# The first transform of u with 64-row, 128-column stationaries, u stored by channels of 640, and one eviction for LN1's shift

## The chip, the cores and the metric

The kernel runs on one core of one Trainium2 chip. The metric is the device time of one execution in microseconds; lower is better. The core has five engines with instruction streams of their own: PE (TensorE, matmuls; its weight loads are listed as PEld), DVE (VectorE), ACT (ScalarE), POOL (GpSimd) and SP (SyncE, which here issues DMAs).

## The reference

u is one sequence of 2048 positions with 640 channels. Two blocks follow each other, each with an adaptive layer norm whose scale, shift and gate come from a condition vector c:

```python
mod = (_silu(c) @ w_mod).reshape(c.shape[0], 6, 1, -1)
sa, ca, ga, sb, cb, gb = (mod[:, i] for i in range(6))
h = _layernorm(x) * (1 + ca) + sa
x = x + ga * _A_ref(h, ...)      # S4: y = irfft(rfft(h) * rfft(K)) + h * Dskip
h = _layernorm(x) * (1 + cb) + sb
x = x + gb * _B_ref(h, w1, w3, w2)   # silu(h w1) * (h w3), times w2
```

K is the convolution kernel of the state space model, `real(sum_n C P dB)` with `P = exp(dt A l)`, for each channel over all 2048 positions. Everything is float32.

## The kernel before, in words

The long convolution is done as a product of transforms. The position is split as l = 64 a + b (a to 32, b to 64), and so is the transform: a first transform over a, for each b, into 32 frequencies f with a real and an imaginary part (64 outputs), then a second over b (`stage2`, line 571, from `uk`), then the product with K's transform, then the inverse. The host lays x out so that a tile of 128 rows holds four values of b, each with its 32 values of a; there are 16 tiles `xt[j]`, j being b // 4.

**The first transform of u** is `u_stage1(j)`, line 395. LN1 has been applied to the tile in place by `ln1_norm` (line 376: statistics on DVE, the root on POOL, one ACT activation for each tile at line 390). LN1's scale 1 + ca is folded into the gate on K's side, so the shift is added as r = sa / (1 + ca); a shift that is constant over a transforms into c1 times r, with c1 the column sums of the transform. Each of the tile's four b, rows 32q to 32q+31, is multiplied with `s1r`, 32 rows by 64 columns, in two halves of 320 channels, so a tile has eight matmuls (line 412), each on an eighth of the array: 32 rows by 64 columns, position (32q, 64 hh). Two PSUM tiles `pu` take the outputs: channel half hh on partitions 64 hh on, two b next to each other in each. `pu[0]` always has the tag Z, of which there is one buffer; `pu[1]` has A or B in turn. The shift is added in one of two ways:

- in `pu[0]` of even tiles, four more matmuls (line 404) of one row, `c1` by `rrow` (r as a row), start the accumulation, and ACT copies the result out (line 415, through `acopy`, line 138);
- in `pu[0]` of odd tiles and in `pu[1]` of all, DVE adds `shift`, c1 times r for all 128 partitions, while it moves the result out (lines 417, 418).

A DMA on SP's queue then stores `u` (two buffers) in `us` in DRAM (line 419), whose layout is [half, c, f, b, 320 channels]; c is the real or the imaginary part. `u_load` (line 550) reads it back into `uk` by blocks of 128 channels, in four parts for each block, with 64 partitions (b) for each c. The third block holds channels 256 to 383, which lie in both halves, so it needs two DMAs where the others need one. For the first block `u_load` is called at step 7 of the loop at line 777, for the others in `stage2`.

**The shift itself** is made in `mod_shift` (line 319), once the first five pieces of the modulation are there (`mod_early`, whose weights `w_mod` come by DMA). Five small DVE instructions give r as columns. Matmuls with the identity (line 330) bring r to 64 rows of `pr` (tag Z), and a DVE copy makes `rrow` (line 331). DVE multiplies c1 with r into columns (line 333), six matmuls turn them (line 339) and a DVE copy makes `shift` (line 341).

**What sets the order.** The program is traced in the order of the code; a planner then orders the instructions of PE and DVE before line 837 by their place and readiness. ACT is different: `act`, `acopy` and `act_set` (lines 133 to 141) keep each ACT instruction behind everything traced on ACT before it, so ACT runs strictly in program order. After `mod_shift` (line 751) come a table load, the exponentials of the first steps (`exps(0)`, `exps(2)`) with `ln1_norm(0)` and `ln1_norm(1)`, and the sines of step 0; tiles 0 to 3 of u come next, and the steps 0 to 5 of the loop at line 777 do two tiles each (line 808), followed by `ln1_norm` of later tiles. In one such step ACT also makes the sines and exponentials of K's tables, DVE multiplies the tables, PE forms K from them (`kgen`, line 522) and transforms it (`k_stage1`, line 540). From line 830 on the order of the convolution is written out by hand. The second block, matmuls listed under the helper line 102, fills the rest of the span.

At the very start SP issues `cT`, `prm` (the parameters), `misc` (small constants, in which also the selectors `selx` and `stepx` lie), `iota`, `ident` and the weights of the modulation, in this order (lines 229 to 236).

Of the kernel before, what the change touches and what calls it, by code (L numbers as in the profile page):

```python
# [17 lines left out]
P = 128  # L18
L = 2048
D = 640  # L20
F = 1728
NA, NB = 32, 64
DC = 128
# [6 lines left out]
KD = D // P  # L30
NFT = 14
WC = 384
# [5 lines left out]
def consts():  # L38

    a = np.arange(NA)[:, None]  # L40
    f1 = np.arange(NA)[None, :]
    ang = 2 * np.pi * a * (f1 + 0.25) / NA
    s1 = np.zeros((4, NA, 2, 4, NA))
    s1r = np.zeros((4, NA, 2, NA))
    for q in range(4):
        s1[q, :, 0, q, :] = np.cos(ang)
        s1[q, :, 1, q, :] = -np.sin(ang)
        s1r[q, :, 0] = np.cos(ang)
        s1r[q, :, 1] = -np.sin(ang)
# [23 lines left out]
    c1 = s1r.reshape(4, NA, 2 * NA).sum(axis=1, keepdims=True).repeat(NA, axis=1).reshape(P, 2 * NA)  # L73
# [5 lines left out]
    misc = np.concatenate([selx, stepx, s1r, c1, one4, toq, tog], axis=1)  # L79
    f = lambda v: np.ascontiguousarray(v, dtype=np.float32)  # L80
    return {"s1": f(s1), "s2": f(s2), "i1": f(i1), "i2": f(i2), "iota": iota, "misc": f(misc),
            "ident": np.eye(P, dtype=np.float32)}
# [25 lines left out]
def tile_kernel(ctx: ExitStack, tc: tile.TileContext, a):  # L108
    nc = tc.nc
    V, S, G, PE = nc.vector, nc.scalar, nc.gpsimd, nc.tensor  # L110

    dram = ctx.enter_context(tc.tile_pool(name="dram", bufs=1, space=DRAM))
    us = dram.tile([2, 2, NA, NB, D // 2], F32, name="us")
    zs = dram.tile([NDC, NB, 2, NA, DC], F32, name="zs")
    xs = dram.tile([NT, P, D], F32, name="xs")

# [1 line left out]
    ident = cp.tile([P, P], F32, name="ident")  # L118
    i2 = cp.tile([P, NA], F32, name="i2")
# [13 lines left out]
    def act(*args, **kw):  # L133

        return tc.keep_in_program_order(S.activation(*args, **kw))  # L135

    def acopy(out, in_):
        return tc.keep_in_program_order(S.copy(out, in_))  # L138
# [18 lines left out]
    s1 = kp.tile([P, 2, P], F32, name="s1")  # L157
    iota = kp.tile([P, NPH], I32, name="iota")
# [7 lines left out]
    uk = kp.tile([P, 3, NA, DC], F32, name="uk")  # L166
# [17 lines left out]
    rrow = pm_.tile([P, D], F32, name="rrow")  # L184
    shift = pm_.tile([P, D // 2], F32, name="shift")
    cols = pm_.tile([P, 7, KD], F32, name="cols")
    lt = pm_.tile([P, 2, D - DC], F32, name="lt")
    misc = pm_.tile([P, 9 * NA + 1 + P], F32, name="misc")
    selx, stepx = misc[:, :NA], misc[:, NA:4 * NA]
    s1r, c1, one4 = misc[:, 4 * NA:6 * NA], misc[:, 6 * NA:8 * NA], misc[:, 8 * NA:8 * NA + 1]  # L190
    toq, tog = misc[:, 8 * NA + 1:8 * NA + 1 + P], misc[:, 8 * NA + 1 + P:]
    tiny = pm_.tile([P, 1], F32, name="tiny")
    V.memset(tiny, -1e-35)

# [31 lines left out]
    d0 = slice(0, DC)  # L226
    d1 = slice(DC, D)
    prma = a["prm"].rearrange("i n d -> n i d")
    nc.sync.dma_start(cT, a["c"])
    S.dma_start(ldt, a["log_dt"].broadcast_to([P, D]))  # L230
    nc.sync.dma_start(prm[:, :, d0], prma[:, :, d0])
# [87 lines left out]
    def mod_shift():  # L319

        sa, ca, ga, zero, inv, r, gs = (cols[:, i] for i in range(7))
        V.tensor_scalar(ca, ca, 1.0, None, op0=OP.add)
        V.tensor_scalar(zero, ca, 0.0, 1e-18, op0=OP.is_equal, op1=OP.mult)
        V.tensor_tensor(ca, ca, zero, op=OP.add)
        V.reciprocal(inv, ca)
        V.tensor_tensor(r, inv, sa, op=OP.mult)

        pr = psS.tile([P, 2, 512], F32, name="pr", tag="Z", bufs=1).rearrange("p a b -> p (a b)")
        for k in range(KD):
            PE.matmul(pr[:64, k * P:(k + 1) * P], r[:, k:k + 1].broadcast_to([P, 64]), ident, start=True, stop=True)  # L330
        V.tensor_copy(rrow[:64], pr[:64, :D])
        rc = pm_.tile([P, WC], F32, name="part", bufs=2)[:, :KD * 2 * NA].rearrange("p (k c) -> p k c", k=KD)
        V.tensor_tensor(rc, bc(c1, 1, KD), bc(r, 2, 2 * NA), op=OP.mult)
        ps = psS.tile([P, 512], F32, name="ps", tag="pk", bufs=1)
        for k in range(KD):
            for hh in range(2):
                lo, hi = max(k * P, hh * 320), min(k * P + P, hh * 320 + 320)
                if lo < hi:
                    PE.matmul(ps[hh * 64:hh * 64 + 64, lo - hh * 320:hi - hh * 320], rc[:, k],
                              ident[:, lo - k * P:hi - k * P], start=True, stop=True, tile_position=(0, hh * 64))  # L340
        V.tensor_copy(shift, ps[:, :320])

    def mod_gate():

# [44 lines left out]
            x = xt[2 * p + i]  # L389
            act(x, x, AF.Identity, scale=rs[:, 1, i:i + 1], bias=rs[:, 2, i:i + 1])  # L390

    usw = us.rearrange("h c f b d -> (h c f) b d")
    usr = us.rearrange("h c f b d -> h c b f d")

    def u_stage1(j):


        x = xt[j]
        u = hpz.tile([P, 4, D // 2], F32, name="u", bufs=2)
        pu = [psS.tile([P, 2, 512], F32, name="pu", tag=t, bufs=1) for t in ("Z", "AB"[j % 2])]  # L400
        one = j % 2 == 0
        for q in range(2 if one else 0):
            for hh in range(2):
                PE.matmul(pu[0][hh * 64:hh * 64 + 64, q, :320], c1[q * NA:q * NA + 1],
                          rrow[q * NA:q * NA + 1, hh * 320:hh * 320 + 320],
                          start=True, stop=False, tile_position=(q * NA, hh * 64))
        for h in range(2):
            for q in range(2):
                r0 = (2 * h + q) * NA
                r = slice(r0, r0 + NA)  # L410
                for hh in range(2):
                    PE.matmul(pu[h][hh * 64:hh * 64 + 64, q, :320], s1r[r], x[r, hh * 320:hh * 320 + 320],  # L412
                              start=not (one and h == 0), stop=True, tile_position=(r0, hh * 64))
        if one:
            acopy(u[:, :2, :], pu[0][:, :, :320])
        else:
            V.tensor_tensor(u[:, :2, :], pu[0][:, :, :320], bc(shift, 1, 2), op=OP.add)
        V.tensor_tensor(u[:, 2:, :], pu[1][:, :, :320], bc(shift, 1, 2), op=OP.add)
        nc.sync.dma_start(usw[:, 4 * j:4 * j + 4, :], u)


    ph, cs, AA, EC, PK, K1 = {}, {}, {}, {}, {}, {}
# [127 lines left out]
    def u_load(ch, i):  # L550

        fs = slice(i * 8, i * 8 + 8)
        for h in range(2):
            lo, hi = max(ch * DC, h * 320), min(ch * DC + DC, h * 320 + 320)
            if lo < hi:
                for c in range(2):
                    nc.sync.dma_start(uk[c * 64:c * 64 + 64, 0, fs, lo - ch * DC:hi - ch * DC],
                                      usr[h, c, :, fs, lo - h * 320:hi - h * 320])

    def stage2(ch, g):  # L560
        s2 = fp.tile([P, 4, P], F32, name="s2", bufs=3)
# [968 lines left out]
```

## Time and profile before

| | us |
|---|---|
| median of 3 runs (lowest, highest) | 968.77 (967.21, 969.94) |
| the profiled execution | 975.08 |
| its span, first to last instruction | 973.3 |
| PE busy | 896.1 (92%) |
| DVE busy | 714.1 (73%) |
| ACT busy | 543.0 (56%) |
| POOL busy | 282.4 (29%) |

The span is one execution; its engines' busy times overlap. PE's share is not a measure of its load in each stage: matmuls that run beside each other on parts of the array are one stretch of busy time, and the clock that TensorE was granted, 0.94 in the mean, is lower in the first 170 us. In the tables by stage the columns are the stretch, its length, busy time (and instructions) of PE, PEld, DVE, ACT and POOL, the granted clock, the share of the DMA engines and GB/s. In lists by time the first two columns are start and length. A bracket names the idle time of an engine before an instruction and what ended it. "128*64 128x256" is a stationary of 128 rows and 64 columns with 256 columns of moving data.

### The profile page before, as it was taken

The page shows a single profiled execution, that of the slowest core. Times are in us where ns is not written, and L with a number is a line of the kernel's source. Part 1 is how long each engine was busy: PE and PEld are TensorE (multiplying, and loading weights), DVE is VectorE, ACT ScalarE, POOL GpSimd, SP SyncE. Part 2 cuts the span into 40 slices and gives each one's busy share as a digit, 9 for nine tenths or more (in the row PEclk, how much of TensorE's full clock was granted, in tenths as well). Part 3 has the DMA queues.
Part 4 walks back from the last instruction along what each step waited for, and adds up shares of the span by engine and source line. Part 5 has one row for each costly group of instructions (what it writes and reads, how often), then busy time and mean ns, then how long its engine had stood idle before and what let it go on. Part 6 is the DMA issues. An engine that isn't in the chain of part 4 may idle for free.

```text
span 973.3 us, 20145 instructions
## 1 busy us (share of the span) xinstructions
PE 896.1 (92%) x7984; PEld 675.4 (69%) x7984; DVE 714.1 (73%) x1259; ACT 543.0 (56%) x795; POOL 282.4 (29%) x278
## 2 busy tenths in 40 slices
PE   4978787889888899899999999999999999999998
PEld 2534444666666666567888888777888888888886
DVE  5598865999999996767666665677786766654675
ACT  4568675999999984236433333455743333333332
POOL 1372343455455641113422220121252222200000
PEclk8555777999999999899999999999999999999999
DMA  9463576655665688785213112895422221113443
GB/s 267 143 228 131 198 202 179 163 147 140 170 162 145 171 224 245 220 216 194 91 55 108 55 55 78 234 272 187 146 84 64 77 66 53 54 41 94 149 150 122
DMA packets 103571, 140.73 MB, mean 145 GB/s; under 512 B 20564, under 2 KB 62676, under 8 KB 103476
## 3 DMA queue, kind: packets, MB, share of 16 engines
q1 hardware_dynamic: 99668, 129.34, 46.0%
q0 software_dynamic: 2304, 7.74, 2.4%
q10 hardware_dynamic: 1504, 2.36, 0.8%
q8 instruction: 63, 1.03, 0.4%
q14 instruction: 32, 0.26, 0.1%
HBM read 107.94 MB, written 31.46 MB: 143 GB/s over the span
## 4 chain that ended last, share of the span: by engine, by line
PE 76%; ACT 9%; DVE 7%; DMA 4%; issue 3%; POOL 0%; ACTq 0%; SPq 0%; DVEq 0%; POOLq 0%
PE ps L102 55%; PE p L571 6%; ACT A L135 3%; PE pz L613 3%; PE pk L522 2%; PE pt L540 2%; ACT cs L135 2%; DMA zs<-zt 2%; PE pq L445 2%; PE pa L435 1%; PE pm L305 1%; PE pu L412 1%; ACT uk L138 1%; DMA uk<-in_w_mod_dram 1%; PE pm L316 1%
## 5 line engine op out<-in xcount | busy, mean ns | idle before, releaser
L102 DVE TENSOR_TENSOR s<-ps,s 128x512 f32<-128x512 f32 x138 | 94.9, 688 | 80.4 <-PE ps L102 79.5
L473 POOL TENSOR_TENSOR ph<-thi,iota 128x1024 int32<-128x1024 int32 x40 | 91.9, 2298 | 154.4 <-DVE A L505 54.0
L102 DVE TENSOR_TENSOR gl<-rw,gh 128x640 fp32r<-128x640 f32 x87 | 78.2, 899 | 65.2 <-ACT gh L102 65.1
L102 ACT CAST gh<-rw 128x640 fp32r<-128x640 f32 x87 | 63.3, 727 | 104.2 <-PE ps L102 63.4
L571 PE MATMUL p<-uk,s 128*64 128x256 f32 x640 | 79.4, 390 | 14.0 <-ACT uk L138 5.8
L102 PE MATMUL ps<-xA,gh 128*128 128x512 f32 x280 | 87.8, 392 | 0.4 <-ACT xA L102 0.4
L102 PE MATMUL ps<-gh,uh 128*128 128x512 f32 x224 | 87.5, 391 | 0.0
L102 PE MATMUL ps<-gl,uh 128*128 128x512 f32 x224 | 87.2, 389 | 0.0
L102 POOL TENSOR_TENSOR S<-rw 128x256 f32<-128x256 f32 x46 | 36.8, 801 | 170.7 <-DVE S0l L102 160.0
L102 PE MATMUL ps<-gh,ul 128*128 128x512 f32 x208 | 81.1, 390 | 0.0
L571 PEld LDWEIGHTS p<-uk,s 128*64 128x64 f32 x640 | 45.9, 139 | 37.8 <-issue 9.7
L498 DVE TENSOR_TENSOR E<-A,cs 128x1024 f32<-128x1024 f32 x40 | 60.4, 1511 | 3.2 <-ACT cs L135 2.5
L102 PEld LDWEIGHTS ps<-xA,gh 128*128 128x128 f32 x280 | 52.1, 188 | 13.0 <-ACT xA L102 0.9
L102 PE MATMUL ps<-xA,gl 128*128 128x512 f32 x140 | 54.6, 390 | 0.0
L474 POOL TENSOR_TENSOR ph<-ph,phi 128x512 int32<-128x512 int32 x40 | 48.5, 1213 | 5.0 <-DVE phi L297 2.0
L540 PE MATMUL pt<-s,K 128*64 128x128 f32 x640 | 48.3, 291 | 1.4 <-ACT uk L138 1.4
L505 DVE TENSOR_TENSOR A<-A,ph 128x1024 f32<-128x1024 f32 x40 | 48.9, 1223 | 0.0
L102 ACT ACTIVATE s<-ps 128x512 f32<-128x512 f32 (+1 forms) x33 | 19.7, 597 | 51.3 <-PE ps L102 51.3
L102 PEld LDWEIGHTS ps<-gl,uh 128*128 128x128 f32 x224 | 42.0, 188 | 9.0
L102 PEld LDWEIGHTS ps<-gh,uh 128*128 128x128 f32 x224 | 42.0, 188 | 8.7
L522 PE MATMUL pk<-E 128*32 128x64 f32 x1280 | 45.9, 233 | 1.5 <-issue 0.9
L613 PE MATMUL pz<-Y,i 64*128 64x128 f32 x640 | 44.4, 282 | 2.8 <-issue 2.7
(255 smaller groups left out, 2270.4 us busy)
## 6 DMA issues: line engine op xcount, KB each, us to landing
rw<-in_w_dram SPq DMA_DIRECT2D x52, 320.0 KB
us<-u SPq DMA_DIRECT2D x16, 640.0 KB
s<-in_s_dram SPq DMA_DIRECT2D x40, 256.0 KB
i<-in_i_dram SPq DMA_DIRECT2D x40, 256.0 KB
rw<-in_wg_dram SPq DMA_DIRECT2D x31, 320.0 KB
rw<-in_wu_dram SPq DMA_DIRECT2D x28, 320.0 KB
uk<-us SPq DMA_DIRECT2D x32, 256.0 KB
zs<-zt SPq DMA_DIRECT2D x32, 256.0 KB
```

What stands on the lines that cost most here:

```text
L102: ins = fn(*args, **kw)
L135: return tc.keep_in_program_order(S.activation(*args, **kw))
L138: return tc.keep_in_program_order(S.copy(out, in_))
L445: keep(PE.matmul(pQ[s][:, rr, :256], w[r, t, :], bc(sel[r, js], 2, NA) if i else r1[r, js, :], start=(i == 0), stop=(i == 1), tile_positio ...
L473: hold(G.tensor_tensor(p, bc(thi[:, sl], 2, NPH), bc(iota, 1, SD), op=OP.mult))
L474: keep(G.tensor_tensor(p[:, :, :NA], p[:, :, :NA], bc(phi[:, sl], 2, NA), op=OP.add))
L498: keep(V.tensor_tensor(EC[s][:, :, 1:3, :], AA[s][:, :, 1:3, :], mid(cs[s]), op=OP.mult))
L505: keep(V.tensor_tensor(A[:, :, 1:3, :], A[:, :, 1:3, :], mid(ph[s]), op=OP.mult))
L522: keep(PE.matmul(pk[dq * 32:dq * 32 + 32, g, :], x[:, g * 4 + dq, 1, :], x[:, g * 4 + dq, 0:3:2, :], start=(st == 0), stop=(st == 1), tile ...
L540: keep(PE.matmul(pt[c * 64:c * 64 + 64, g, :], kk[:, g, :], s1[:, c, :], start=True, stop=True, tile_position=(0, c * 64)))
L571: keep(PE.matmul(p2[par * 64:par * 64 + 64, pi, c, :], s2[:, pi * 2 + par, c * 64:c * 64 + 64], uk[:, 0:kn + 1:kn, f, :], start=True, stop ...
L613: ins = keep(PE.matmul(pz[:, par, (g % 2) * 2 + pi, :], i1[r, pi, c, :], Y[r, pi, c, :], start=(c == 0), stop=(c == 1), tile_position=(par ...
```

## The change

- The stationary of a tile's transform becomes `s1b`: for a half of the tile (two b, 64 rows) a block diagonal matrix of 64 rows and 128 columns, the first b into outputs 0 to 63 and the second into 64 to 127. A tile has four data matmuls in place of eight; `pu[t]` holds half t, with all 640 channels beside each other in two banks.
- In all tiles `pu[0]` takes the shift by matmuls, two of one row (`c1` by a row of `shift`, 128 columns), and is copied by ACT; in all tiles `pu[1]` takes it by a DVE addition.
- `mod_shift` brings r to all 128 partitions, and one ACT activation scales it by c1 as it leaves PSUM. `rrow`, the DVE multiplication and the turning matmuls go.
- `us` is [c, f, b, 640 channels]. A tile is stored by two DMAs of 64 partitions, one for each b of a pair. A part of a block is read by two DMAs for every block.
- `selx` and `stepx` move from `misc` to a tensor of their own, `selstep`, loaded ahead of `cT`.

```diff
-    us = dram.tile([2, 2, NA, NB, D // 2], F32, name="us")
+    us = dram.tile([2, NA, NB, D], F32, name="us")
...
+    selx, stepx = selstep[:, :NA], selstep[:, NA:]
+    s1b, c1, c1c, one4 = misc[:, :P], misc[:, P:2 * P], misc[:, 2 * P:2 * P + 1], misc[:, 2 * P + 1:2 * P + 2]
...
+    nc.sync.dma_start(selstep, a["selstep"])
     nc.sync.dma_start(cT, a["c"])
...
         for k in range(KD):
-            PE.matmul(pr[:64, k * P:(k + 1) * P], r[:, k:k + 1].broadcast_to([P, 64]), ident, start=True, stop=True)
-        V.tensor_copy(rrow[:64], pr[:64, :D])
...
-        V.tensor_copy(shift, ps[:, :320])
+            PE.matmul(pr[:, k * P:(k + 1) * P], r[:, k:k + 1].broadcast_to([P, P]), ident, start=True, stop=True)
+        act(shift, pr[:, :D], AF.Copy, scale=c1c)
...
-    usw = us.rearrange("h c f b d -> (h c f) b d")
-    usr = us.rearrange("h c f b d -> h c b f d")
+    usw = us.rearrange("c f (j t i) d -> i (c f) j t d", t=2, i=2)
+    usr = us.rearrange("c f b d -> c b f d")
...
-        u = hpz.tile([P, 4, D // 2], F32, name="u", bufs=2)
+        u = hpz.tile([P, 2, D], F32, name="u", bufs=2)
         pu = [psS.tile([P, 2, 512], F32, name="pu", tag=t, bufs=1) for t in ("Z", "AB"[j % 2])]
-        one = j % 2 == 0
-        for q in range(2 if one else 0):
+        for hh in range(2):
+            PE.matmul(pu[0][:, hh, :320], c1[:1], shift[:1, hh * 320:hh * 320 + 320], start=True, stop=False,
+                      tile_position=(0, 0))
+        for t in (1, 0):
+            r = slice(t * 64, t * 64 + 64)
             for hh in range(2):
...
+                PE.matmul(pu[t][:, hh, :320], s1b[r], x[r, hh * 320:hh * 320 + 320], start=(t == 1), stop=True,
+                          tile_position=(r.start, 0))
+        split = lambda v: v.rearrange("p (h d) -> p h d", h=2)
+        acopy(split(u[:, 0]), pu[0][:, :, :320])
+        V.tensor_tensor(split(u[:, 1]), pu[1][:, :, :320], split(shift), op=OP.add)
+        for i in range(2):
+            nc.sync.dma_start(usw[i, :, j], u[i * 64:i * 64 + 64])
...
+        for c in range(2):
+            nc.sync.dma_start(uk[c * 64:c * 64 + 64, 0, fs], usr[c, :, fs, ch * DC:ch * DC + DC])
```

More of the change, by code (lines that the diff above doesn't have):

```diff
@@ L71, in consts @@
     stepx = np.concatenate([np.arange(NB), 64 * np.arange(NA)])[None].repeat(P, 0)
-    c1 = s1r.reshape(4, NA, 2 * NA).sum(axis=1, keepdims=True).repeat(NA, axis=1).reshape(P, 2 * NA)
+    s1b = np.zeros((4, NA, 2, 2 * NA))
+    for q in range(4):
+        s1b[q, :, q % 2] = s1r[q * NA:(q + 1) * NA]
+    s1b = s1b.reshape(P, P)
+    c1 = np.tile(s1r[:NA].sum(axis=0), 2)
     one4 = (np.arange(P) % NA == 0).astype(np.float32)[:, None]
@@ L183, in tile_kernel @@
     scb = pm_.tile([P, KD, NA], F32, name="scb")
-    rrow = pm_.tile([P, D], F32, name="rrow")
-    shift = pm_.tile([P, D // 2], F32, name="shift")
+    shift = pm_.tile([P, D], F32, name="shift")
     cols = pm_.tile([P, 7, KD], F32, name="cols")
     lt = pm_.tile([P, 2, D - DC], F32, name="lt")
[L188 to L191, printed above, removed]
+    misc = pm_.tile([P, 3 * P + 2 + NA], F32, name="misc")
+    selstep = pm_.tile([P, P], F32, name="selstep")
+    selx, stepx = selstep[:, :NA], selstep[:, NA:]
+    s1b, c1, c1c, one4 = misc[:, :P], misc[:, P:2 * P], misc[:, 2 * P:2 * P + 1], misc[:, 2 * P + 1:2 * P + 2]
+    toq, tog = misc[:, 2 * P + 2:3 * P + 2], misc[:, 3 * P + 2:]
     tiny = pm_.tile([P, 1], F32, name="tiny")
@@ L329, in mod_shift @@
         for k in range(KD):
-            PE.matmul(pr[:64, k * P:(k + 1) * P], r[:, k:k + 1].broadcast_to([P, 64]), ident, start=True, stop=True)
-        V.tensor_copy(rrow[:64], pr[:64, :D])
[L332 to L340, printed above, removed]
-        V.tensor_copy(shift, ps[:, :320])
+            PE.matmul(pr[:, k * P:(k + 1) * P], r[:, k:k + 1].broadcast_to([P, P]), ident, start=True, stop=True)
+        act(shift, pr[:, :D], AF.Copy, scale=c1c)
     def mod_gate():
@@ L552, in u_load @@
         fs = slice(i * 8, i * 8 + 8)
[L553 to L558, printed above, removed]
+        for c in range(2):
+            nc.sync.dma_start(uk[c * 64:c * 64 + 64, 0, fs], usr[c, :, fs, ch * DC:ch * DC + DC])
     def stage2(ch, g):
```

21 lines of the change are left out of this document (3 added, 18 removed).

## The prediction

> **What bounds the kernel now.** I read first the table by stage (busy us of each engine in a stretch of the span, granted TensorE clock, share of the DMA engines), since the page's 92% of PE is a mean over unlike stages.
>
> ```profile
> span 973.3 us, 20145 instructions
> ...
> 41.00:129.00 88.00, 71.95 (x810) 37.39 (x806) 78.17 (x140) 64.29 (x77) 38.95 (x39) 0.62 0.47 169
> 400.00:973.00 573.00, 563.61 (x2724) 454.31 (x2720) 380.89 (x674) 240.10 (x416) 114.10 (x150) 0.99 0.39 116
> ```
>
> The columns are PE, PEld, DVE, ACT, POOL, clock, DMA share, GB/s. After 400 us PE is the bound and nothing there is edited. The first transform of u lies in 41 to 129: DVE is busy for 78.17 of 88 us, PE for 71.95 at a clock of 0.62, ACT for 64.29, DMA for 0.47. No engine is full, so a chain that passes between them sets the time. What follows needs u in memory, so a delay of 129 us delays the end by as much. Second view, the chain of waits of that stretch, by line:
>
> ```profile
> by line: PE pu L412 13.3%; issue 8.8%; DVE u L418 6.1%; ACT x L135 5.9%; PE pk L522 5.8%; ACT A L135 5.0%; ACT cs L135 4.6%; PE pu L404 4.0%; DVE st L383 3.3%; DVE A L509 3.1%; DVE E L498 3.0%; PE pt L540 2.9%; PE pq L445 2.7%; DVE A L505 2
> ```
>
> The transform's matmuls are 17.3% of it (15.2 us), the DVE additions of line 418 6.1% (5.4 us). Third, the instructions that write `pu` and `u` (minimum, median and maximum ns):
>
> ```profile
> L412 PE MATMUL pu<-x,misc x256: 425/736/792, 41.2 to 127.3; 32*64 32x320 f32 x128
> ...
> L404 PE MATMUL pu<-rrow,misc x64: 427/736/791, 39.2 to 121.4; 1*64 1x320 f32 x64
> L418 DVE TENSOR_TENSOR u<-pu,shift x16: 806/813/825, 43.8 to 127.1; 128x640 f32<-128x640 f32 x16
> L138 ACT COPY u<-pu x8: 669/692/694, 47.8 to 124.4; 128x640 f32<-128x640 f32 x8
> L417 DVE TENSOR_TENSOR u<-pu,shift x8: 810/818/825, 52.2 to 128.1; 128x640 f32<-128x640 f32 x8
> ```
>
> A matmul leaves two records here (16 tiles of 8 make 256). Fourth, PE in order of time for two tiles, at clock 0.5:
>
> ```profile
> 62.81 1.34 PE L404 MATMUL pu<-rrow,misc 1*64 1x320 f32 x8 [1.52 <-DVE u L417]
> 63.55 1.68 PE L412 MATMUL pu<-x,misc 32*64 32x320 f32 x14
> 66.04 1.35 PE L412 MATMUL pu<-x,misc 32*64 32x320 f32 x10 [0.81 <-ACT u L138]
> 67.32 0.44 PE L522 MATMUL pk<-E 128*32 128x64 f32 x8
> ```
>
> The tile at 66.04 has eight matmuls on eight different eighths of the array, and all take 1.35 us together: they run abreast, one level. The tile at 62.81 has a bias level before it and is done at 65.23: two levels, 2.42 us, so each further level costs 1.07.
>
> **The change, part by part.** The sum is against the profiled execution (975.08 us, span 973.3); that lies 6.3 over the median of 968.77, so I add the differences to the median.
>
> *Matmuls of u.* Per tile now 8, and 4 more on even tiles: 1 or 2 levels, on average (1.35+2.42)/2 = 1.88 us at half clock. New: 6 matmuls 128 columns wide, of the same 320 columns of moving data. The two bias matmuls sit on the same rows and columns, so they are two levels; the two data matmuls of a half are two more; the halves can run abreast. Four levels: 1.35+3*1.07 = 4.56 us; five, 5.63, if the second half starts one level late because it is issued behind both matmuls of the first. Fewer instructions, but 2.4 to 3 times the array time: 0.94 us a tile at full clock become 2.28 to 2.82, over 16 tiles 21.4 to 30.1 more. In the stage PE has 71.95*0.62 = 44.6 full-clock us now; it gets 66 to 75 in 88.
>
> Does the bias run beside the data of rows 64 to 127? Above it overlaps (63.55 lies before 64.15), but there both have the shape 32*64; pk, 128*32, starts at 67.32, only 0.07 before pu is modelled to end. [...]
>
> *Evictions.* Eight DVE additions (818 ns) go, eight ACT copies (692) come: DVE 78.2 to about 71.6 us, ACT 64.3 to 69.8. On the chain a third of line 418's 5.4 us goes: 2 us gained. Dearer is the order. `pu[0]` is always tag Z, one buffer, and ACT's instructions stand in program order (line 135); now both tiles of a step leave Z through ACT, one directly behind the other:
>
> ```profile
> 65.29 0.69 ACT L138 COPY u<-pu 128x640 f32<-128x640 f32 x1 [4.21 <-PE pu L412]
> 67.21 1.74 ACT L135 ACTIVATE x<-x,rs 128x640 f32<-128x640 f32 x2 [1.23 <-DVE rs L387]
> ...
> 77.99 1.73 ACT L135 ACTIVATE x<-x,rs 128x640 f32<-128x640 f32 x2 [3.31 <-DVE rs L387]
> ```
>
> After the first copy the second tile's bias may start; the second copy waits for all its levels, 2.28 us at full clock, 4.56 at half, and behind it stand LN1's `x`, the next step's table load, exponentials and sines, and PE and DVE wait for those. Per pair ACT has 69.8/8 = 8.7 us of work: with the stall 11.0 at full, 13.3 at half clock, 88 to 106 us for eight pairs against 88 now. ACT's waits of today (3.31 before `x` at 77.99) partly run beside the new one. I take a clock of 0.8: 2.85 us of stall, 92.6 us, +4.6, and 1.4 for waits not covered: **+6** (bounds 0 and 18). At 0.8 PE's 66 us are 83 of 88, so its gaps close too: **+3** (bounds -5 and 15).
>
> *The shift.* Five matmuls now 128 columns wide stay at 2.40 us; twelve records (1.76) and three DVE instructions (1.75) go; one ACT activation 128x640 comes, no row of its own: between the copy's 0.69 and half of LN1's 1.73 (two of them); I take 0.8. It stands in ACT's order behind the cast at 18.39, ahead of the exponentials:
>
> ```profile
> 18.39 0.37 ACT L138 CAST lm<-pT 128x256 fp32r<-128x256 f32 x1 [1.30 <-PE pT L291]
> ...
> 39.34 0.60 ACT L135 ACTIVATE A<-pq 128x512 f32<-128x512 f32 x1 [1.79 <-PE pq L445]
> 41.31 0.60 ACT L135 ACTIVATE A<-pq 128x512 f32<-128x512 f32 x1 [1.38 <-PE pq L445]
> ...
> 43.43 1.04 ACT L135 ACTIVATE cs<-ph 128x1024 f32<-128x1024 int32 x1
> ```
>
> ```profile
> 34.62 2.40 PE L330 MATMUL pr<-ident,cols 128*64 128x128 f32 x10 [2.43 <-DVE cols L326]
> 36.81 1.76 PE L339 MATMUL ps<-ident,part 128*64 128x128 f32 x12
> ```
>
> ```profile
> 18.78:43.43 24.65, 22.22 (x124) 13.57 (x123) 9.46 (x30) 10.79 (x13) 7.62 (x8) 0.50 0.60 192
> ```
>
> Its input is ready at 37.0, where line 330's matmuls end; or up to 3 us sooner, an estimate: PE is busy for 22.22 of these 24.65 us, partly with pq and pa, which no longer come between. From 34.8 to 37.8 (0.8 for the activation) ACT then has what it now does from 18.78 to 43.43: 10.8 us busy (the window's ACT column) and at least 3.2 of waits for PE (1.79 and 1.38). It reaches the `cs` of 43.43 at 49 to 52, 5 to 9 later. Idle time that ACT has behind it and the removed rows take some: **+3** (bounds 0 and 9).
>
> *Memory.*
>
> ```profile
> 0.74 0.39 SPq L229 DMA_DIRECT2D cT<-in_c_dram  x1
> 1.19 0.42 SPq L231 DMA_DIRECT2D uk<-in_prm_dram  x1
> ```
>
> ```profile
> L557 SPq DMA_DIRECT2D uk<-us x48: 579/627/2291, 133.8 to 372.9; - x48
> L419 SPq DMA_DIRECT2D us<-u x16: 319/326/858, 48.5 to 128.9; - x16
> ```
>
> `selstep` is issued ahead of `cT` and `prm`, and costs them an issue (0.39, 0.42) and a little of the transfer: **+0.5**. Stores of u become two of half size: 16 issues more, 5.3 us of SP over 80, beside the work; bytes as before. Packets halve to 2560 bytes; at a share of 0.47 I count nothing (bounds 0 and 2). Loads of u: 40 instead of 48, since the third block no longer straddles two halves; that block is read after 163.5, off the chain: nothing (bounds -2 and 0).
>
> Sum: 0.5+3+6+3-2 = **+10.5**, so 968.8+10.5 = 979.3, rounded **979**.
>
> **The rivals.**
> *Full clock, faster.* The clock of stretches of 3.41 us:
>
> ```profile
> 43.35:46.76 3.41, 3.41 (x27) 1.28 (x20) 2.92 (x8) 3.38 (x4) 0.00 (x0) 0.50 0.00 0
> 46.76:50.17 3.41, 2.52 (x22) 1.11 (x20) 3.20 (x3) 1.70 (x3) 3.27 (x3) 1.00 0.26 108
> 67.24:70.65 3.41, 3.41 (x69) 2.26 (x64) 3.41 (x5) 3.41 (x6) 0.00 (x0) 0.50 0.93 373
> 70.65:74.07 3.42, 2.01 (x46) 1.19 (x42) 3.42 (x9) 3.39 (x5) 2.27 (x2) 0.50 0.99 325
> 115.03:118.44 3.41, 2.15 (x24) 1.24 (x24) 3.13 (x5) 1.75 (x3) 1.25 (x3) 1.00 1.13 342
> 118.44:121.85 3.41, 1.51 (x27) 0.81 (x32) 2.83 (x6) 2.63 (x3) 0.55 (x1) 1.00 0.46 184
> 121.85:125.27 3.42, 1.49 (x20) 0.22 (x3) 3.42 (x4) 3.39 (x6) 3.06 (x2) 0.50 0.48 194
> ```
>
> A filled stretch can raise the next (46.76), though not each does (70.65); at 1.00 PE keeps it at 2.15 busy and loses it after 1.51. More work fills more stretches; if the stage then stays at 1.00, the other matmuls on the chain (pk, pt, pq: 11.4%, 10 us) halve: -5; u's 15.2 us grow by 2.28/1.88: +3; DVE's -5.8 counts whole; ACT's stalls are covered; the shift gives -1.5 and `selstep` +0.5. About -9: **960**. It decides from the point where PE stays over some 2 us busy in each 3.4. [...] Against it: the stall of ACT leaves PE idle too.
> *Half clock throughout.* 66 to 75 at 0.62 are 107 to 121 us: +19 to +33, with the shift **996**. [...]
> *Nothing comes through.* Stalls run beside today's waits, DVE's gain pays for the front: **969**.
>
> **How the numbers follow.** Forecast 0.48 (own range 972 to 988), full clock 0.22, half clock 0.18, nothing 0.12. Reaching into both sides until 2 in 10 are left out: 958 to 998. About 0.3% (2.9 us) can be told from no change: faster 0.21, same 0.13, slower 0.66.
>
> **What would show it.** Right: ACT idle from about 18.8 to 34 or later, before the activation that makes `shift`; 4.5 or 2.3 us from a tile's first bias matmul to its last, by clock; second copies of a pair waiting for pu; a clock of about 0.8 in the stage; 16 DVE additions. Wrong: first matmuls of line 571 starting before 163.5; a clock near 1.00 from 50 on with the chain on DVE; bias and data matmuls overlapping so that a tile takes three levels; or the load of `uk` at the stage's end getting later through smaller packets.

## The result and the profile after

The change made the kernel slower, by far more than forecast.

| | before | after |
|---|---|---|
| time, median (lowest to highest) of 4 runs | 969.36 us (967.21 to 970.02) | 1027.85 us (1023.4 to 1036.36) |
| ratio, 95% interval | | 1.0618 (1.0547 to 1.0689) |
| profiled execution: time, span | 975.08, 973.3 us | 1023.4, 1021.6 us |
| first matmul of the second transform (`p<-uk`) starts at | 163.45 us | 211.71 us |

The last row places the loss: 211.71 - 163.45 = 48.3 us, which is the whole difference of the spans. Before that matmul lies the first transform of u; behind it the two executions run alike. The granted clock in tenths, for 40 slices of the span, from the page of before:

```profile
PEclk8555777999999999899999999999999999999999
```

The page of after (slices of 25.5 us) and its table by stage (PE, PEld, DVE, ACT, POOL, granted clock, DMA share, GB/s; the stage of 88 us before now lasts some 136):

```profile
span 1021.6 us, 19896 instructions
...
PEclk9555556899999999989999999999999999999999
```

```profile
41.00:129.00 88.00, 82.44 (x478) 46.69 (x478) 58.50 (x108) 45.45 (x58) 28.18 (x32) 0.54 0.38 104
80.00:100.00 20.00, 20.00 (x178) 12.09 (x176) 9.05 (x13) 8.82 (x12) 2.95 (x2) 0.57 0.49 129
41.00:179.00 138.00, 129.03 (x751) 74.34 (x747) 75.70 (x133) 67.10 (x84) 37.71 (x39) 0.56 0.38 106
```

The second to sixth slice, 25 to 153 us, stand at 5; before had 7 in its fifth to seventh. In 41 to 129 us PE rose from 71.95 to 82.44 us of 88, while DVE fell from 78.17 to 58.50 and ACT from 64.29 to 45.45: two engines have room, one is nearly full. From 80 to 100 PE never stops, and is still granted 0.57 of its clock; 14.39 of these 20 us are the transform's own streams, the rest mostly those that form and transform K (`pk`, `pt`). The chain of waits of after, 41 to 180 us, by line, says the same:

```profile
by line: PE pu L403 32.3%; PE pu L398 17.6%; PE pk L512 9.1%; PE pt L530 7.3%; issue 2.6%; DVE E L488 2.6%; DVE A L495 2.5%; PE pT L297 2.1%; PE pq L435 2.1%; DVE st L379 1.7%; POOL ph L463 1.7%; DVE A L499 1.3%; DVE u L407 1.2%; DVE uk L25
```

The transform's matmuls (data, line 403, and bias, line 398) are 49.9% of 139 us, 69 us; they were 15.2 before. The instructions on `pu` and `u` (minimum, median, maximum ns):

```profile
L403 PE MATMUL pu<-x,misc x128: 429/737/899, 41.3 to 179.8; 64*128 64x320 f32 x128
...
L398 PE MATMUL pu<-shift,misc x64: 427/736/897, 31.4 to 178.5; 1*128 1x320 f32 x64
L407 DVE TENSOR_TENSOR u<-pu,shift x16: 761/818/825, 51.8 to 178.4; 128x640 f32<-128x640 f32 x16
L143 ACT COPY u<-pu x16: 669/692/692, 53.9 to 180.3; 128x640 f32<-128x640 f32 x16
```

The evictions are as forecast, 16 DVE additions and 16 ACT copies at unchanged durations. The median matmul record is no longer than before either (737 ns, before 736). The difference is how many stand one behind another. A level, below, is one matmul, or several that run abreast in the time of one. PE of after in order of time:

```profile
53.18 2.50 PE L403 MATMUL pu<-x,misc 64*128 64x320 f32 x4
55.61 2.50 PE L398 MATMUL pu<-shift,misc 1*128 1x320 f32 x4
...
66.92 2.47 PE L403 MATMUL pu<-x,misc 64*128 64x320 f32 x4 [0.68 <-DVE u L407]
...
71.18 2.50 PE L398 MATMUL pu<-shift,misc 1*128 1x320 f32 x4
73.61 2.51 PE L403 MATMUL pu<-x,misc 64*128 64x320 f32 x8
76.89 2.50 PE L398 MATMUL pu<-shift,misc 1*128 1x320 f32 x4 [0.77 <-ACT u L143]
79.31 2.50 PE L403 MATMUL pu<-x,misc 64*128 64x320 f32 x4
```

Two matmuls (x4 records) take 2.5 us; the granted clock was 0.50 in 53 to 58 us and in 66 to 83. At 66.92 one half of a tile runs alone, 4.3 us ahead of the bias at 71.18; at 76.89 a bias, then at 79.31 its half. Only in a few places, as at 73.61 (x8 in 2.51), two halves run abreast. The likely reason, argued from the code and not shown: the planner places an instruction where its buffers are free, `pu[1]` has tags A and B and comes free early, `pu[0]` waits for Z; so the halves, written as neighbours, are issued apart. Most tiles are six levels, not the four or five of the forecast. PE's busy time in `pu` alone, before and then after (PE, PEld, DVE, ACT, clock, DMA share, GB/s):

```profile
31.00:180.00 149.00, 37.31 (x320) 12.30 (x320) 19.42 (x24) 5.47 (x8) 0.70 0.54 172
```

```profile
31.00:180.00 149.00, 96.08 (x192) 48.42 (x192) 13.05 (x16) 10.34 (x15) 0.56 0.40 113
```

There are fewer matmuls, and PE is busy with them for 58.8 us more.

### The profile page after: what moved, and what is told of

It is laid out like the page before. It is cut to its first block, busy times and chain, and to the rows that moved or that the text cites. A ratio compares the mean times of both kernels' runs of the same rounds, so it can differ in the third digit from the quotient of the medians.

```text
span 1021.6 us, 19896 instructions
## 1 busy us (share of the span) xinstructions
PE 950.4 (93%) x7844; PEld 709.9 (69%) x7844; DVE 709.5 (69%) x1248; ACT 548.6 (54%) x804; POOL 276.4 (27%) x278
## 4 chain that ended last, share of the span: by engine, by line
PE 77%; ACT 8%; DVE 5%; DMA 5%; issue 3%; SPq 1%; POOL 1%; DVEq 0%; ACTq 0%; POOLq 0%
PE ps L107 49%; PE p L557 6%; PE pu L403 4%; PE pz L599 3%; PE pk L512 3%; PE pt L530 3%; PE pu L398 3%; DMA A<-zs 3%; ACT A L140 2%; ACT cs L140 2%; DMA uk<-in_w_mod_dram 2%; PE pm L311 2%; PE pq L435 1%; SPq L107 1%; PE pa L425 1%
## 5 line engine op out<-in xcount | busy, mean ns | idle before, releaser
L403 PE MATMUL pu<-x,misc 64*128 64x320 f32 x128 | 60.9, 723 | 1.9 <-ACT lm L143 1.1
L530 PE MATMUL pt<-s,K 128*64 128x128 f32 x640 | 51.3, 297 | 3.3 <-ACT uk L143 2.2
L403 PEld LDWEIGHTS pu<-x,misc 64*128 64x128 f32 x128 | 31.3, 307 | 28.0 <-issue 18.7
L512 PE MATMUL pk<-E 128*32 128x64 f32 x1280 | 48.5, 237 | 1.0 <-DVE K L520 1.0
```

The lines of the kernel that those rows point to most:

```text
L403: PE.matmul(pu[t][:, hh, :320], s1b[r], x[r, hh * 320:hh * 320 + 320], start=(t == 1), stop=True, tile_position=(r.start, 0))
L512: keep(PE.matmul(pk[dq * 32:dq * 32 + 32, g, :], x[:, g * 4 + dq, 1, :], x[:, g * 4 + dq, 0:3:2, :], start=(st == 0), stop=(st == 1), tile ...
L530: keep(PE.matmul(pt[c * 64:c * 64 + 64, g, :], kk[:, g, :], s1[:, c, :], start=True, stop=True, tile_position=(0, c * 64)))
```

## The experiments

**Theory P:** the six levels, at half clock, bind the stage; the rest hides behind them. **Rival M:** the memory layout, with two stores a tile, binds. **Rival S:** ACT is held at the start by the shift. **Rival E:** the evictions' engine and order bind. Every time is a median, and every ratio is to runs of before on the same chip (medians 969.4 to 971.3 us); only e12's interval holds 1. To compare, "`pu`" is PE's busy time in the transform's matmuls from 31 to 180 us, and "start" the start of the first `p<-uk` matmul; both are of one execution. In e4 and e13 a few of these matmuls lie behind 180 us and are not counted.

| kernel | median us | ratio to before (95%) | `pu` us | start us |
|---|---|---|---|---|
| after | 1027.85 | 1.0547 to 1.0689 | 96.08 | 211.71 |
| e1, after: no bias | 984.03 | 1.0105 to 1.0166 | 52.73 | 176.47 |
| e2, after: halves abreast | 1012.65 | 1.0390 to 1.0473 | 69.23 | 199.27 |
| e5, after: bias of 64 rows | 1010.76 | 1.0371 to 1.0426 | 80.53 | 199.16 |
| e6, after: all streams 128 rows | 996.01 | 1.0234 to 1.0297 | 65.30 | 185.64 |
| e4, after: shift by DVE | 1036.52 | 1.0663 to 1.0708 | 95.87 | 221.60 |
| e13, after: x loads ahead | 1030.50 | 1.0567 to 1.0676 | 96.83 | 214.76 |
| e15, no bias, abreast | 995.47 | 1.0197 to 1.0294 | 46.23 | 184.79 |
| e14, e15 with x loads ahead | 982.94 | 1.0092 to 1.0148 | 38.35 | 171.80 |
| e16, e14 with shift by DVE | 981.47 | 1.0077 to 1.0137 | 37.01 | 167.39 |
| e18, e16 with streams of 128 rows | 985.63 | 1.0104 to 1.0178 | 50.07 | 172.03 |
| e20, e16 with one store a tile, to other places | 983.72 | 1.0095 to 1.0170 | 44.58 | 173.13 |
| e3, before: new layout | 998.73 | 1.0251 to 1.0338 | 40.00 | 184.53 |
| e9, before: two stores a tile | 998.49 | 1.0233 to 1.0331 | 39.92 | 184.74 |
| e11, e3 with x loads ahead | 984.87 | 1.0095 to 1.0181 | 38.87 | 173.45 |
| e12, before: x loads ahead | 968.97 | 0.9961 to 1.0016 | 38.05 | 158.51 |
| e7, before: ACT and bias in all tiles | 989.01 | 1.0135 to 1.0228 | 47.88 | 176.08 |
| e19, before: no bias, DVE alone | 979.60 | 1.0064 to 1.0145 | 33.08 | 167.68 |
| e8, before: shift by ACT | 979.65 | 1.0075 to 1.0125 | 42.35 | 174.69 |

### TensorE's streams: e1, e2, e5, e6

e1 takes the bias out, and with it ACT's copies:

```diff
-            PE.matmul(pu[0][:, hh, :320], c1[:1], shift[:1, ...], start=True, stop=False, tile_position=(0, 0))
...
-        acopy(split(u[:, 0]), pu[0][:, :, :320])
+        V.tensor_tensor(split(u[:, 0]), pu[0][:, :, :320], split(shift), op=OP.add)
```

> The changed kernel without the one-row bias matmuls: DVE adds the shift in both halves, ACT copies nothing out of pu. Theory (array time: the levels of a tile run one behind another at half clock, and PE is the chain): 16 tiles lose two levels of 1.07 to 1.2 us each, 24 us of them on the chain, so 1028 - 25 to 40 = 988 to 1003, still 20 or more above the kernel before. Second theory (one-row matmuls keep the clock down): the granted clock from 41 us to the end of the transform rises well over 0.56, and the time falls below 988. Rival (ACT's order: two copies of the one-buffer tag Z behind each other): with the copies gone all of the difference goes, 970.

e2 keeps the bias and issues the four data matmuls behind it, halves alternating:

```diff
-        for t in (1, 0):
-            for hh in range(2):
+        with tc.issue_after(bias.ins):
+            for hh in range(2):
+                for t in (1, 0):
...
```

> The changed kernel with the four data matmuls of a tile issued together behind its bias, the halves in turn, so that rows 0-63 and 64-127 run side by side in every tile. Array time theory: about 11 of 16 tiles save two levels of 1.07 us, so 1028 - 23 = about 1005. Clock theory (streams that use half of the array or one row do not raise the clock): more stretches with both halves in use, clock over 0.65, under 1000. Rival (ACT's order): no change, 1028, since the copies stand as they did.

e5 gives the bias the shape of the data, e6 gives every stream all 128 rows:

```diff
-  PE.matmul(pu[0][:, hh, :320], c1[:1], shift[:1, ...], start=True, stop=False, tile_position=(0, 0))
+  PE.matmul(pu[0][:, hh, :320], c1[:64], shift[:64, ...], start=True, stop=False, tile_position=(0, 0))
```

```diff
-  PE.matmul(pu[t][:, hh, :320], s1b[r], x[r, ...], start=(t == 1), stop=True, tile_position=(r.start, 0))
+  PE.matmul(pu[t][:, hh, :320], s1z[:, t * P:t * P + P], x[:, ...], start=(t == 1), stop=True)
...
```

> After, with the bias matmul of shift taken over 64 rows (63 of them zero) instead of one, so that it has the shape of the data matmuls and lies on the rows that the second half's don't use. [...] Theory B (the bias stands alone because of the order alone, or the serial streams don't bind): 1022 to 1036 us, as after.

> After, with each half's stationary padded by zeros to 128 rows and the bias taken over 128 rows (127 of them zero): six streams of the whole array one behind another for each tile, nothing abreast. Theory A (the stage is bound by TensorE's streams at a granted clock of 0.5 to 0.6, and streams of half the rows or of one row don't raise that clock): the granted clock over 41 to 129 us rises to 0.8 or more, a stream falls from 1.25 to 0.6 us for most, and the time falls to 965 to 1000 us. Theory B (the clock doesn't depend on the rows in use): the clock stays at 0.5 to 0.6, and the time is that of after or above, 1022 to 1045 us.

All four came down: by 44, 15, 17 and 32 us against after's median. e1 gained more than its first theory allowed (988 to 1003), but not as the second said: without any one-row stream the clock over 41 to 129 us was only 0.60. e2 gained less than the 23 us expected, and its clock there was 0.60 too. Still, e2 removes levels (`pu` 96.08 to 69.23), with the same evictions, stores and shift: levels bind. In e5 the bias no longer always stands alone. In its order of time a bias and a half on the other rows start together:

```profile
94.00 0.53 PE L398 MATMUL pu<-shift,misc 64*128 64x320 f32 x1
94.01 0.53 PE L403 MATMUL pu<-x,misc 64*128 64x320 f32 x1
94.37 0.43 PE L398 MATMUL pu<-shift,misc 64*128 64x320 f32 x1
94.39 0.43 PE L403 MATMUL pu<-x,misc 64*128 64x320 f32 x1
```

In after, the two halves behind the bias of 71.18 start only at 73.61, when its two matmuls are over (modelled to end at 73.68), though one of them lies on the other 64 rows. No bias of after, one row by 128 columns, starts less than 0.35 us from a data matmul; in e5, with 64 rows, they are 0.01 us apart. So it was not the order alone that kept the bias by itself: e5's 1010.76 us lie under the 1022 of its Theory B. Nor was it the one row alone: in before a bias of one row and 64 columns (the prediction calls its shape 32*64, its records say 1*64) starts 0.06 us from data of 32 rows and 64 columns:

```profile
98.13 0.81 PE L404 MATMUL pu<-rrow,misc 1*64 1x320 f32 x4 [0.34 <-DVE u L417]
98.19 0.80 PE L412 MATMUL pu<-x,misc 32*64 32x320 f32 x3
```

What held the bias of after apart, no run shows.

e6 has six levels in every tile and nothing abreast, yet is 32 us faster than after, since its clock is another. Its table by stage, then three rows of PE:

```profile
41.00:129.00 88.00, 71.64 (x616) 45.51 (x618) 65.92 (x122) 56.83 (x72) 36.60 (x37) 0.88 0.48 133
```

```profile
70.30 1.65 PE L399 MATMUL pu<-shift,misc 128*128 128x320 f32 x4
71.79 2.32 PE L403 MATMUL pu<-x,misc 128*128 128x320 f32 x8
73.94 1.24 PE L399 MATMUL pu<-shift,misc 128*128 128x320 f32 x4
```

The clock is 0.88 in place of 0.54, and four records take 1.24 us in place of 2.50. The rows added to the stationaries hold zeros, so the results are the same. In after, streams of half the array, or of one row, made up 14.39 of the 20.00 busy us from 80 to 100, which were granted no more than 0.57.

Could the one-row bias alone hold the clock down? e5 has none, every stream of its transform has 64 rows, and two matmuls still take 2.50 us there:

```profile
86.61 2.50 PE L398 MATMUL pu<-shift,misc 64*128 64x320 f32 x4
88.91 2.34 PE L403 MATMUL pu<-x,misc 64*128 64x320 f32 x4
```

So it is not the one row. The durations are the evidence for e5, not its table, which gives 0.84 for 41 to 129 us and 1.00 for 41 to 98: its trace has no record of the clock before about 94 us, and the table counts such time as full clock. (Of the four runs of after, the slowest, 1036.36 us, lists a mean clock of 0.977, the others 0.915 to 0.923. The same gap may be the reason; its trace was not kept.) e5 and e6 have the same six streams a tile but for their rows, 64 and 128; whether the rows or the share of the array in use counts, no run separates.

### The layout in memory: e3, e9, e11, e12, e13

e3 puts only the new layout of `us` into before; a tile of old shape needs two stores for it (64 partitions by 4 by 320), and blocks are read whole:

```diff
-        nc.sync.dma_start(usw[:, 4 * j:4 * j + 4, :], u)
+        for h in range(2):
+            nc.sync.dma_start(usw[:, 4 * j:4 * j + 4, h * 320:h * 320 + 320], u[h * 64:h * 64 + 64])
```

> The kernel before with only the layout of u in memory changed (channels of 640, two stores of 64 partitions for each tile, 40 loads in place of 48). Array time theory: memory is off the chain, 969 within 3. Rival (smaller packets or the queue of SP): 975 or more, with the loads of uk at the end of the preamble later. If the third block's whole packets were worth something: 966 or less.

It lost 28 us. The expected rival came (975 or more), dearer than its bound suggested, and with two reasons in it, packets and queue. e9 keeps the old layout and only halves the stores:

```diff
-        nc.sync.dma_start(usw[:, 4 * j:4 * j + 4, :], u)
+        for h in range(2):
+            nc.sync.dma_start(usw[h * 64:h * 64 + 64, 4 * j:4 * j + 4, :], u[h * 64:h * 64 + 64])
```

> Before, its layout in memory kept, with the one edit that the store of a tile of u is two stores of 64 partitions. Theory A (two stores a tile double SP's entries, and the order that is planned for SP then puts the loads of x behind stores that wait for u): the whole loss of the run with the new layout on the old tiles, 994 to 1003 us, first stage2 matmul at 183 to 186 us. Theory B (the layout itself costs: places of u further apart in memory, loads of whole blocks): no change, 966 to 974 us.

e9 loses as much (998.49), so it is not the places in memory but the second store. SP's queue in order of time, before and then e9:

```profile
48.48 4.89 SPq L419 DMA_DIRECT2D us<-u  x2
53.46 1.34 SPq L374 DMA_DIRECT2D x<-in_x_dram  x2
58.85 5.00 SPq L419 DMA_DIRECT2D us<-u  x2
63.94 1.34 SPq L374 DMA_DIRECT2D x<-in_x_dram  x2
```

```profile
44.71 14.67 SPq L420 DMA_DIRECT2D us<-u  x6
59.47 0.87 SPq L374 DMA_DIRECT2D x<-in_x_dram  x1
63.31 11.61 SPq L420 DMA_DIRECT2D us<-u  x6
75.02 0.87 SPq L374 DMA_DIRECT2D x<-in_x_dram  x1
79.27 5.02 SPq L420 DMA_DIRECT2D us<-u  x4
84.38 23.60 SPq L374 DMA_DIRECT2D x<-in_x_dram  x7
```

With twice the stores the planner found another order: six stores, each waiting for its eviction, and one load of x behind them. Seven of the nine tiles of x that were not loaded at the start are asked for only from 84.38 on. ACT's wait for LN1's statistics in 41 to 160 (total, times, longest), before and then e9:

```profile
ACT x L135 <- DVE rs L387: 10.4, 5, 3.3
```

```profile
ACT x L135 <- DVE rs L387: 22.9, 3, 14.8
```

e11, e12 and e13 put the load of tile j+7 ahead of the stores of tile j, in fixed order, into e3, before and after:

```diff
+        if j + 7 < NT:
+            ln1_load(j + 7)
         for h in range(2):
-            nc.sync.dma_start(usw[...], u[h * 64:h * 64 + 64])
+            tc.keep_in_program_order(nc.sync.dma_start(usw[...], u[h * 64:h * 64 + 64]))
```

> The new layout on the tiles of before (two stores of 64 partitions a tile, 40 whole loads), with the load of x tile j+7 put on SP's queue ahead of the stores of tile j, in a fixed order. Theory A (loads of x stand behind stores): it comes back to 964 to 980 us, first stage2 matmul at 163 to 172 us. Theory B (the layout itself) and theory C (the issue time of 16 more stores on SP): as with the new layout alone, 994 to 1003 us.

> Before, with the load of x tile j+7 put on SP's queue ahead of the store of tile j, in a fixed order: the control of the run above. All theories: within 6 us of before, 963 to 975 us, since the planned order of before already has each load of x ahead of the stores of its time.

> After, with the load of x tile j+7 put on SP's queue ahead of the two stores of tile j, in a fixed order. Theory A (loads of x behind stores are one part of the loss, and the serial streams on TensorE the other): 15 to 30 us less than after, 997 to 1012 us. Theory D (the serial streams of bias, first and second half at half clock bind the stage alone, PE being busy through 80 to 100 us): no change, 1022 to 1036 us.

In e11 half of the 28 us came back and 14 stayed, which no theory had; before did not care; and after, where the same order would have helped by M, did not move (1030.5). M is real on the old tiles, and its part that lies in the order of the loads is hidden in after: PE is the later of the two.

### The shift: e4, e8

```diff
-        act(shift, pr[:, :D], AF.Copy, scale=c1c)
+        V.tensor_scalar(shift, pr[:, :D], c1c, None, op0=OP.mult)
```

> The changed kernel with shift made by one DVE multiplication in place of the ACT activation, so that ACT is not held behind mod_shift. Array time theory: the later stage is bound by PE, so at most the few us that ACT is late at its start come back, 1020 to 1028. Rival (ACT's order at the start): 10 or more come back, under 1018.

Undone in after, it gains nothing: 1036.5 is slower still. S falls as the cause of the loss. e8 puts it into before:

```diff
...
-        V.tensor_copy(shift, ps[:, :320])
+        for hh in range(2):
+            act(shift[hh * 64:hh * 64 + 64], pr[hh * 64:hh * 64 + 64, hh * 320:hh * 320 + 320], AF.Copy, scale=...)
```

> Before, with only its shift made the new way: six matmuls of 128 rows broadcast, and ScalarE making the shift in two evictions of 64 partitions (before: VectorE's two copies, one product and seven small matmuls). Theory of the prediction (the shift stands in ScalarE's order ahead of the exponentials): 3 us, up to 9, slower than before: 970 to 980 us. Rival (ScalarE's later start is covered): 966 to 972 us.

There it costs 8.6 us (1.0075 to 1.0125). (The two kernels make the shift with five matmuls of `r`; the turning ones that go are six.) ACT in e8, whose activation has to wait for a DVE copy of the same PSUM tile too:

```profile
37.74 1.06 ACT L135 ACTIVATE shift<-pr,misc 64x320 f32<-64x320 f32 x2 [18.86 <-DVE rrow L332]
...
55.90 1.04 ACT L135 ACTIVATE cs<-ph 128x1024 f32<-128x1024 int32 x1
```

The first `cs` is 12.5 us later than before (43.43). In after it is 6.1 later:

```profile
30.57 0.79 ACT L140 ACTIVATE shift<-pr,misc 128x640 f32<-128x640 f32 x1 [11.32 <-PE pr L336]
...
49.51 1.04 ACT L140 ACTIVATE cs<-ph 128x1024 f32<-128x1024 int32 x1
```

### The evictions: e7, e19

ACT of after, the second copy of a pair, and its waits for `pu` in 41 to 179 us (total, times, longest):

```profile
60.57 0.69 ACT L143 COPY u<-pu 128x640 f32<-128x640 f32 x1 [6.03 <-PE pu L403]
```

```profile
ACT u L143 <- PE pu L403: 49.4, 12, 9.2
```

Before alternates: ACT with bias in even tiles, DVE in odd ones. e7 sets `one = True`, e19 `one = False`.

> Before, with the bias matmuls and ScalarE's copy for the first half of every tile (before: of every second tile; VectorE adds the shift in the others). The prediction's term for ScalarE's evictions and the order they take, 6 us of 0 to 18, says 975 to 982 us, less VectorE's relief of 2. Rival (the eviction's engine doesn't matter): 966 to 973 us. Rival (one-row bias matmuls are streams of their own on TensorE, at half clock, 2.5 us for each tile more): up to 990 us.

> Before, without any bias matmul and without ScalarE's copies: VectorE adds the shift in both evictions of every tile (before: of every second tile). Theory A (each tile with one-row bias streams costs TensorE a level at half clock, and ScalarE's copy waits for it: 8 tiles more cost 19 us): 8 tiles fewer give some of it back, 955 to 968 us. Theory B (VectorE, busy for 78 of 88 us there, becomes the bound with 8 evictions more, 6.5 us): 972 to 980 us.

Both are slower: 19 and 9 us. In e7, with the narrow matmuls of before, eight tiles more have a bias level, and ACT's copy waits for the transform's matmuls; before and then e7, in 41 to 160:

```profile
ACT u L138 <- PE pu L412: 6.0, 2, 4.2
```

```profile
ACT u L138 <- PE pu L412: 30.2, 9, 5.0
```

The forecast's term for the evictions (975 to 982) is missed here; the expected rival with streams of their own, up to 990, fits.

In e19 `pu` is down to 33.08 us and DVE, with 8 evictions more, is late with LN1 (`x` waits 20.6 us for `rs`, 10.4 before). Theory A of e19 failed and B came: neither more nor fewer copies on ACT than half and half was faster, and the change gives that up. E is thus a cost of its own; but e2, e5 and e6 keep every eviction of after and are 15 to 32 us faster than it, so in after ACT mostly waits for the streams, and not the streams for ACT.

### What is left without the streams: e14, e15, e16, e18, e20

e15 is e1 with the halves alternating; e14 adds the x loads ahead; e16 the shift by DVE; e18 pads the stationaries of e16 with zeros; e20 writes each tile of e16 with one store.

```diff
...
+        first_mm = mm(0, 0)
+        with tc.issue_after(first_mm.ins):
+            mm(1, 0)
+            mm(0, 1)
+            mm(1, 1)
```

> After without the bias matmuls (VectorE adds the shift in both evictions) and with the halves of a tile issued alternately, the loads of x left where the planner puts them. If the order of x loads is what still costs once TensorE's streams don't bind: 990 to 1000 us, 10 or so more than with the loads ahead (982.94). If the loads don't matter even then: 978 to 988 us.

> After, without the bias matmuls (VectorE adds the shift in both halves' evictions, ScalarE copies none), the two halves of a tile issued alternately so that they run abreast, and the load of x tile j+7 on SP's queue ahead of the stores of tile j. If the serial streams and the loads behind stores are the whole loss: 960 to 975 us, before or a little less. If something else of the change costs (selstep's load at the start, the shift on ScalarE, VectorE's larger share of evictions): 976 to 990 us.

> The run without bias, halves abreast and x loads ahead, and the shift made by one VectorE operation instead of ScalarE's activation. Theory A (what is left, 12 us over before, is ScalarE held by the shift at the start, as in the run that put that edit alone into before and lost 9): 970 to 977 us. Theory B (what is left lies with the two stores a tile, or with VectorE's 32 evictions): 979 to 988 us.

> The same, with each half's stationary padded by zeros to 128 rows, so that a tile is four streams of the whole array one behind another in place of two pairs abreast. Theory A (streams of the whole array raise the granted clock, and at full clock four in a row, 4 x 0.55 us, cost no more than two levels at half clock): the clock over 41 to 129 us at 0.8 or more against 0.70, time 962 to 975 us, the best of the new layout, perhaps under before. Theory B (the stage now hangs on VectorE or on the stores): the same as without the padding, within 4 us.

```diff
-        for i in range(2):
-            tc.keep_in_program_order(nc.sync.dma_start(usw[i, :, j], u[i * 64:i * 64 + 64]))
+        tc.keep_in_program_order(nc.sync.dma_start(usx[:, j], u.rearrange("p t d -> p (t d)")))
```

> The run without bias, with halves abreast, x loads ahead and VectorE's shift, where each tile of u goes to memory in one store of 128 partitions, to places that are not those that the loads of u expect (the order of u in memory is left wrong, so the output is not the reference's; the bytes, loads and everything behind are the same). Theory A (the 11 us that stay over before are the second store of a tile, 1.24 us of SP for a pair against 0.33): 965 to 974 us. Theory B (they are not the stores): 977 to 986 us.

Once PE no longer binds, the x loads count: e14 lies 12.5 us under e15. The shift's engine then does not: e16 and e14 have overlapping intervals. Nor does the store: e20 is not under e16. Nor does more clock: e18's is 0.83 in 41 to 129 us, e16's 0.72, and e18's time is no lower.

```profile
41.00:129.00 88.00, 64.78 (x584) 40.69 (x584) 78.85 (x142) 54.14 (x64) 34.91 (x37) 0.83 0.54 150
```

In e18 DVE is busy for 78.85 of 88 us there and PE for 64.78. What stays over before is about 11 us in e16 and 9 in e19, with overlapping intervals, and these two share DVE's 32 evictions; that fits, but no run took the 32 out of e16 with the rest kept, so it is argued, not shown. No version beat before; e12 cannot be told from it.

## Why the prediction was wrong

The direction was right, for a reason the forecast gave too little weight. Its steps:

- **"I take a clock of 0.8"** is the step that failed. The stage got 0.54 to 0.57. The work was sized well: "it gets 66 to 75" full-clock us, and 129.03 us of PE at 0.56 in 41 to 179 are 72.3. At 0.8 that would be 90 us, about the old stage; at the granted 0.56 it took 129. So the term "its gaps close too" (+3, bounds -5 and 15) is the one mis-sized: relieving PE gave back 32 us with all else kept (e6), and 44 with the bias and ACT's copies gone (e1). The 0.8 was the author's estimate, and neither before (0.62 in 41 to 129) nor after shows it for this stage: from 80 to 100 us of after PE was busy for 20.00 of 20 us and was granted 0.57. Nor does the full-clock rival's point of some 2 us busy in each 3.4 hold: before, at 1.00, had PE busy for 2.52 us in 46.76 to 50.17, and the next stretch, to 53.59, was granted 0.50. e6 beside e5 shows what was missing: two matmuls of 128 rows took 1.24 us (e6, at 73.94), two of 64 rows 2.50 (e5, at 86.61). The clock is not the whole of it: e6, at 0.88, still lies 25 us over before (996.01 against 971.02), more than twice the 10.5 of the sum, and no run separates what its levels, evictions and stores cost there.
- **Four levels, or five**: mostly six, because the planner separated the halves, and because no bias of after started within 0.35 us of data. The first was not foreseen: the forecast read the code's order as PE's order. The second the text put as a question; in e5, with 64 rows, the bias started 0.01 us from data. `pu` took 96.08/16 = 6.0 us a tile, where 4.56 to 5.63 were forecast at half clock (and 37.31/16 = 2.3 us before, where the forecast reckoned 1.88).
- **The rival "half clock throughout" (996)** was the mechanism that came. Its own sum, 107 to 121 us in place of 88, is +19 to +33, and the measured 48 lies beyond by the levels and by 0.56 in place of 0.62.
- **The evictions (+6, bounds 0 and 18)**: the wait named was there: ACT's second copy of a pair, at 60.57 us, waits 6.03 us for `pu`, and ACT's wait for `pu` in 41 to 179 is 49.4 us in 12 times. Alone in before it costs 19 (e7). The 2 us counted for DVE's relief came to nothing: DVE fell to 58.50 us of 88 and was not late.
- **The shift (+3, bounds 0 and 9)**: the place was right (`cs` later by 6.1; "5 to 9 later" was said), though the activation began at 30.57, sooner than the 34 to 37 reckoned. Alone in before, in another form, it costs 8.6 us; in after, undoing it brought nothing back (e4).
- **`selstep` (+0.5)** was not tried alone; it is still in e16, whose whole rest is 11 us.
- **Memory ("beside the work", nothing)**: wrong as a price. 16 stores more cost before 27 to 28 us (e9, e3). Their time on SP was more than the 5.3 us reckoned (in e3 32 stores with a median of 608 ns, some 19 us, in place of 16 with 326, some 5), but half of the loss came back with the loads of x in another order (e11): each store can wait, and the loads were planned behind them. The forecast counted the issues and not the queue's new order. In after that order adds nothing that could be measured (e13).

The losses do not add up: 19 (e7), 28 (e3) and 9 us (e8) alone in before, and the levels beside them, make 58 together, since a delay off the latest chain is covered. What stays open is the 14 us of e11 with the x loads ahead (a pair of stores holds SP for 1.24 us, a single one for 0.33, yet on the new tiles one store in place of two gained nothing), and why e4 is slower than after: its planned order differs in more than the shift.

## What to carry to other kernels

Count matmuls by levels, that is by what can stand beside what in the order in which the scheduler really issues them, and not by number: fewer, wider matmuls were 2.6 times the time here. Do not price a stage at a clock that it has not yet shown. Where a planner orders a queue, a transfer split in two is a new plan: look for what now stands behind an entry that waits, and put loads ahead of it by hand.

## What the runs showed of the hardware

- From 80 to 97 us of after PE was busy for 17.00 us, 12.46 of them with the transform's streams of 64 rows or of one row, and the granted clock was 0.50. The same six streams a tile padded to 128 rows (e6) were granted 0.88 in 41 to 129 us, and took 1.24 us for two matmuls at 73.94, in place of 2.50. With 64 rows and no one-row stream (e5) two matmuls at 86.61 still took 2.50.
- In after no bias of one row and 128 columns started less than 0.35 us from a stream of 64 rows; of 64 rows, with 63 of zeros (e5), it started 0.01 us apart from one. In before one of one row and 64 columns started 0.06 us from a stream of 32 rows (98.13 and 98.19).
